# Expert stage of a fused attention, MoE and FFN kernel: queue of the output writes, place of row loads, inner job sizes and banks

## Chip, cores and metric

One core of a Trainium2 chip. The metric is the device time of one execution in microseconds (us). The kernel before takes 1082.27 us, the median of three runs (1080.63 to 1087.08). Engines: TensorE (PE) multiplies matrices, VectorE (DVE), ScalarE (ACT) and GpSimd (POOL) work on elements, SyncE (SP) issues transfers (DMAs); ScalarE and GpSimd can issue them too. Each engine runs its own list of instructions in order and waits on semaphores for the others.

## What is computed

Attention with a window of 128 and 4 sink tokens over 4 x 8 heads of 768 x 64 gives 3072 tokens of 512 values. Each token goes to one of 8 experts, and a second FFN follows:

```python
def _moe_ref(x, w_gate, w1, w2):
    expert_idx = np.argmax(x @ w_gate, axis=1)
    ...  # gate_w: the softmax probability of that expert
    for e in range(8):
        mask = expert_idx == e
        xe = x[mask]
        h = np.maximum(xe @ w1[e], 0.0)          # 512 -> 1024
        out[mask] = gate_w[mask, None] * (h @ w2[e])   # 1024 -> 512
def _moe2_ref(x, w_in, w_out):
    h = x @ w_in                                  # 512 -> 2048
    return (h - np.tanh(h)) @ w_out
```

## The kernel before

Every float32 operand is split into a high and a low float16 half, and a product is three float16 matmuls (`mm3`, L663 to L665).

**Three stages.** Stage A, to about 225 us, is the attention; its rows are scattered by expert into a DRAM tensor `bucket`. Stage B, to about 571 us, runs the experts (`stage_b`). Their outputs go to a DRAM tensor `yc`, ordered by expert, together with the token numbers. Stage C, to the end, runs the FFN over `yc` in six groups of 512 rows; `load_y` (L1041) loads a group transposed into `y`, its token numbers into `idf`.

**Stage B** takes the experts in order of their counts as seen before the last batch, and expert x below is the x-th of that order. Each has a main job over its first rows, `FIRST` = 256 rows for experts 0 to 5 and 128 for 6 and 7. A job is `job()`: layer 1 in blocks of one PSUM bank, each evicted by ScalarE (`h` high, L773) and VectorE (`h` low, L774), then layer 2 into one bank per 128 rows, evicted by L788 and L789, then the output write. The remaining rows are counted in units of 64 and cut into inner jobs under conditionals whose registers are loaded from the table `ctl` (L676): `half` of 64 rows (`half_job`, layer 2 at L813 and L814), `odd` of 128 rows, `jobs` of 256 rows and, behind the first of those, a loop for more. The half and the odd job of an expert run inside its main job's layer 1 (for experts 0 and 1 inside the main jobs of 1 and 2), a 256-row job behind it. The last rows of an expert may be computed twice by overlapping jobs, which write the same values.

**The order around the jobs** is written by hand. `plan(p, f)` puts a step at hook p, and `job` calls `hook(-1)` ahead of its first block, then one hook after each block of layer 1 and each of 8 steps of layer 2. Steps are: register reads and row loads for the next expert (`first`, `decide`, `further_rows`, at the places in `AHEAD`), weights of the next expert (raw chunks `stg` loaded by SyncE, L695 and L699; converted and split by `prep`: L713 on ScalarE, then either L719 on VectorE or L721 and L722 on POOL), pieces of the FFN's weights (`w64_prep`, L742 to L752), and the first `load_y`, at hook `YAT[1]` of expert 6. `both` calls the hook's steps ahead of the inner half or odd job of that place. All stores to `yc` and all row loads are issued by SyncE, in the program's order. A store to `yc` and a later load of it, or the reverse, wait for each other, since the rows are known only at run time.

**Banks.** A main job uses s0 to s3 and pt, pt; a 256-row inner job `MORE` = s1, s2, s3, s0 and oa, ob for layer 2; half and odd jobs `PART` = oa, ob and s0. `soon` gives TensorE a hint on the next branch.

## Time and profile before

| | before |
|---|---|
| median of 3 runs | 1082.27 us |
| profiled execution | 1082.43 us |
| its span | 1080.7 us |
| busy: TensorE, VectorE, ScalarE, GpSimd | 91%, 49%, 40%, 41% |
| mean granted TensorE clock | 0.971 |
| expert stage | about 225 to 571 us |

The span runs from the first to the last instruction. A clock of 1.00 is 2.4 GHz and 0.50 is 1.2 GHz. In rows of a timeline the bracket tells how long the engine was idle before the instruction and which engine, line or transfer released it; `DVEq` or `PEq` is an engine's sequencer (branches, registers), `issue` means that nothing in the trace explains the wait.

### The profile page before, as it was taken

The page shows a single profiled execution, that of the slowest core. Times are in us where ns is not written, and L with a number is a line of the kernel's source. Part 1 is how long each engine was busy: PE and PEld are TensorE (multiplying, and loading weights), DVE is VectorE, ACT ScalarE, POOL GpSimd, SP SyncE. Part 2 cuts the span into 40 slices and gives each one's busy share as a digit, 9 for nine tenths or more (in the row PEclk, how much of TensorE's full clock was granted, in tenths as well). Part 3 has the DMA queues.
Part 4 walks back from the last instruction along what each step waited for, and adds up shares of the span by engine and source line. Part 5 has one row for each costly group of instructions (what it writes and reads, how often), then busy time and mean ns, then how long its engine had stood idle before and what let it go on. Part 6 is the DMA issues. An engine that isn't in the chain of part 4 may idle for free. (4 is left out here: it accounts for less than half of the span.)

```text
span 1080.7 us, 19260 instructions
## 1 busy us (share of the span) xinstructions
PE 986.9 (91%) x6883; PEld 581.0 (54%) x6883; DVE 526.4 (49%) x1188; ACT 428.3 (40%) x1178; POOL 439.7 (41%) x595
## 2 busy tenths in 40 slices
PE   7799878778976999998878999999999999999996
PEld 6688767655654656665543444444444444444442
DVE  6588786846224548574625988352052053043000
ACT  5687776733232334333414563252052043043000
POOL 5777878846203245243412553143143043033010
PEclk9999998998997999999998999999999999999998
DMA  7967788586719877693654415202002000000000
GB/s 195 236 175 202 194 226 229 177 188 220 147 50 268 198 191 220 166 245 127 149 91 81 85 53 147 78 11 49 30 1 50 20 10 11 20 10 1 30 31 20
DMA packets 152264, 125.13 MB, mean 116 GB/s; under 512 B 108800, under 2 KB 121088, under 8 KB 152128
## 3 DMA queue, kind: packets, MB, share of 16 engines
q1 hardware_dynamic: 141616, 94.26, 35.8%
q0 software_dynamic: 8160, 28.34, 8.2%
q8 instruction: 76, 1.25, 0.5%
q10 hardware_dynamic: 2352, 0.79, 0.4%
q14 instruction: 60, 0.49, 0.1%
HBM read 75.98 MB, written 23.79 MB: 92 GB/s over the span
## 5 line engine op out<-in xcount | busy, mean ns | idle before, releaser
L1071 DVE SCALAR_TENSOR_TENSOR w<-z 128x512 f32<-128x512 f32 x96 | 72.6, 756 | 219.7 <-ACT z L1069 215.7
L1059 POOL TENSOR_TENSOR gl<-w,gh 128x512 f16<-128x512 f32 x96 | 117.8, 1228 | 145.6 <-ACT gh L1058 145.2
L663 PE MATMUL s<-y,wi 128*128 128x512 f16 x384 | 146.4, 381 | 6.8 <-DMA y<-yc 6.8
L665 PE MATMUL s<-y,wi 128*128 128x512 f16 x384 | 146.3, 381 | 0.0
L664 PE MATMUL s<-y,wi 128*128 128x512 f16 x384 | 146.3, 381 | 0.0
L663 PE MATMUL pt<-wo,gh 128*128 128x512 f16 x352 | 133.4, 379 | 0.0
L665 PE MATMUL pt<-wo,gl 128*128 128x512 f16 x352 | 133.4, 379 | 0.0
L664 PE MATMUL pt<-wo,gh 128*128 128x512 f16 x352 | 133.4, 379 | 0.0
L1069 ACT ACTIVATE z<-s 128x256 f32<-128x256 f32 x192 | 71.8, 379 | 112.2 <-PE s L665 111.5
L225 PE MATMUL s<-kf,qz 128*128 128x264 f32 (+2 forms) x384 | 100.0, 385 | 3.9 <-DVEq L1279 2.9
L1092 POOL DMA_INDIRECT out_dram<-ot,idu x24 | 23.5, 981 | 196.1 <-ACT ot L1091 186.4
L244 ACT ACTIVATE P<-P,mn 128x264 f32<-128x264 f32 (+1 forms) x192 | 93.6, 489 | 19.5 <-DVE mn L236 18.1
L1091 ACT ACTIVATE ot<-pt 128x512 f32<-128x512 f32 x22 | 13.1, 597 | 194.5 <-PE pt L665 184.7
L731 POOL DMA_DIRECT2D w<-in_w_dram x30 | 16.9, 563 | 149.9 <-DVE f L744 135.6
L225 PEld LDWEIGHTS s<-kf,qz 128*128 128x128 f32 x384 | 66.5, 200 | 11.4 <-PEq L1279 3.2
L1072 DVE SCALAR_TENSOR_TENSOR w<-s,w 128x512 f32<-128x512 f32 x96 | 66.4, 691 | 10.0
L236 DVE CUSTOM_DVE_ANT_0 P<-s,mask 128x264 f32<-128x264 f32 (+1 forms) x192 | 69.5, 396 | 0.9 <-PE s L225 0.6
L268 ACT CAST PT<-pt 128x512 f16<-128x512 f32 (+1 forms) x96 | 52.2, 543 | 36.9 <-PE pt L262 36.5
L663 PEld LDWEIGHTS <-wi 128*128 128x128 f16 x384 | 37.7, 98 | 52.9 <-DVEq L920 7.2
L262 PE MATMUL pt<-ident,P 128*128 128x128 f32 x352 | 60.2, 291 | 6.2 <-DVE PT L274 3.8
L1058 ACT CAST gh<-w 128x512 f16<-128x512 f32 x96 | 59.2, 617 | 11.5 <-DVE w L1072 11.5
L665 PEld LDWEIGHTS <-wi 128*128 128x128 f16 x384 | 37.7, 98 | 45.8 <-issue 1.0
(267 smaller groups left out, 2246.7 us busy)
## 6 DMA issues: line engine op xcount, KB each, us to landing
stg<-in_w_dram SPq DMA_DIRECT2D x64, 512.0 KB
w<-in_w_dram POOLq DMA_DIRECT2D x30, 512.0 KB, 4.4
kf<-in_kT_dram SPq DMA_DIRECT2D x16, 396.0 KB
qz<-in_qT_dram SPq DMA_DIRECT2D x32, 192.0 KB
vf<-in_vP_dram SPq DMA_DIRECT2D x16, 384.0 KB
xf<-xg SPq DMA_DIRECT2D x48, 128.0 KB
row<-hl SPq DMA_DIRECT2D x15, 384.0 KB
yc<-y SPq DMA_DIRECT2D x10, 514.0 KB
```

The source lines that it names most:

```text
L225: nc.tensor.matmul(ps[:, c0:264], lhsT=u.qf[h][:, qc], rhs=u.kf[:, kc], start=True, stop=True, skip_group_check=True)
L236: nc.vector.tensor_tensor_reduce(out=u.P[i // 2][:, it % 4, c0:], in0=s[h][:, c0:264], in1=e.M[:, min(i, 2), c0:], op0=ALU.add, op1=ALU.mi ...
L244: nc.scalar.activation(p, p, AF.Exp, scale=-1.0, bias=u.mn[:, it:it + 1], accum_out=u.sums[:, it:it + 1])
L262: nc.tensor.transpose(ps[:, j], u.P[i // 2][:, it % 4, c0:c0 + 128], e.ident)
L663: nc.tensor.matmul(out, lhsT=lh, rhs=rh, start=start, stop=False)
L664: nc.tensor.matmul(out, lhsT=lh, rhs=rl, start=False, stop=False)
L665: nc.tensor.matmul(out, lhsT=ll, rhs=rh, start=False, stop=stop)
L1058: nc.scalar.copy(gh[:, f], w)
L1059: nc.gpsimd.tensor_tensor(gl[:, f], w, gh[:, f], op=ALU.subtract)
L1069: nc.scalar.activation(z[:, s], p[:, s], AF.Square, scale=1.0 / (YS * WIS), accum_out=e.zsum[:, n:n + 1])
L1071: nc.vector.scalar_tensor_tensor(w, z, -2.5, z, op0=ALU.add, op1=ALU.mult)
L1072: nc.vector.scalar_tensor_tensor(w, p, -2.0 / 15.0 * G2 / (YS * WIS), w, op0=ALU.mult, op1=ALU.mult)
```

## The change

Outputs of the jobs are written by ScalarE's queue (`queue=nc.scalar`), those inside loops still by SyncE; ScalarE therefore reads the registers of the output's place too (`IO`). Expert 2's first rows are loaded in `late`, in job 1, and for later experts at hook 0 of the job before (`AHEAD`). Half job 0 stands at hook 7 of job 1 instead of 5. The steps of a hook come behind the inner job of that place. Experts 4 to 7 (`FEW`) have no 256-row case: their remaining rows are a half job and as many 128-row jobs as needed, from the second on in a loop inside `odd`. Inner 256-row jobs use s2, s3, oa, ob and pt, pt. The first `load_y` stands at hook 1 of expert 6 instead of hook 12. The copy of gate and token number comes before the output's evictions.

```diff
@@ -476,7 +476,8 @@
     nc.vector.tensor_scalar(e.ctl[:, 3], ci[:, 1], 2, None, op0=ALU.logical_shift_right)
-    nc.vector.tensor_scalar(e.ctl[:, 4], ci[:, 1], 1, 1, op0=ALU.logical_shift_right, op1=ALU.bitwise_and)
+    nc.vector.tensor_scalar(e.ctl[:, 4, 0:FEW], ci[:, 1, 0:FEW], 1, 1, op0=ALU.logical_shift_right, op1=ALU.bitwise_and)
+    nc.vector.tensor_scalar(e.ctl[:, 4, FEW:], ci[:, 1, FEW:], 1, None, op0=ALU.logical_shift_right)
     nc.vector.tensor_scalar(e.ctl[:, 8], ci[:, 1], 1, None, op0=ALU.bitwise_and)
@@ -641,14 +642,14 @@
 INNER = "hi", 2
-MORE, PART = (["s1", "s2", "s3", "s0"], ["oa", "ob"]), (["oa", "ob"], ["s0"])
+MORE, PART = (["s2", "s3", "oa", "ob"], OUT), (["oa", "ob"], ["s0"])
 TAIL = [1, 3, 6, 7, 8]
...
 AT = [3, 5]
-YAT = 2, 12
+YAT = 2, 1
 WHEN = [0.0, 0.7, 0.06, 0.7]
 LATER = 0, 256
-AHEAD = [3, 5, 7, 9]
+AHEAD = [0, 5, 6, 7]
 FETCH = (64, 128, 256), (256, 64, 128), (64, 128, 256)
@@ -657,6 +658,10 @@
 ET = mybir.EngineType
+IO = ET.SP, ET.Activation
+FEW = 4
@@ -783,11 +788,11 @@
         e.x64.tile([128, 1, ROW], F16, tag="yo", name="yo", bufs=2)
+    nc.vector.tensor_copy(yr.bitcast(F32)[:, 0:nt, 512:514], g.bitcast(F32)[:, 0:nt])
     for t in range(nt):
...
         nc.vector.scalar_tensor_tensor(yr[:, t, 512:1024], ys[t], gt, yr[:, t, 0:512], op0=ALU.mult, op1=ALU.subtract)
-    nc.vector.tensor_copy(yr.bitcast(F32)[:, 0:nt, 512:514], g.bitcast(F32)[:, 0:nt])
     write(yr)
@@ -815,11 +820,11 @@
     y, gt = yr[0:64, 0], g.bitcast(F32)[0:64, 0, 0:1]
+    nc.vector.tensor_copy(yr.bitcast(F32)[0:64, 0, 512:514], g.bitcast(F32)[0:64, 0])
     nc.scalar.copy(yf, ys[64:128])
...
     nc.vector.scalar_tensor_tensor(y[:, 512:1024], yf, gt, y[:, 0:512], op0=ALU.mult, op1=ALU.subtract)
-    nc.vector.tensor_copy(yr.bitcast(F32)[0:64, 0, 512:514], g.bitcast(F32)[0:64, 0])
     write(yr)
@@ -844,39 +849,39 @@
-    def write(base, start, T):
+    def write(base, start, T, queue=nc.scalar):
         row = nc.s_assert_within(base + start, 0, YROWS - T, skip_runtime_bounds_check_because=WHY)
...
             p = min(T, 128)
-            nc.sync.dma_start(e.yc[bass.ds(row, T), :].rearrange("(t p) c -> p t c", p=p), yr[0:p, 0:T // p].bitcast(U16))
+            queue.dma_start(e.yc[bass.ds(row, T), :].rearrange("(t p) c -> p t c", p=p), yr[0:p, 0:T // p].bitcast(U16))
         return f
...
         for n in names:
-            row, engines, top = dict(n=(1, (ET.SP,), 3072), base=(2, (ET.SP,), 3072), jobs=(3, None, 12),
-                                     odd=(4, None, 1), done=(5, (ET.SP,), 256), s1=(6, (ET.SP,), 3072 - 256),
-                                     so=(7, (ET.SP,), 3072 - 128), half=(8, None, 1), sh=(9, (ET.SP,), 3072 - 64))[n]
+            row, engines, top = dict(n=(1, (ET.SP,), 3072), base=(2, IO, 3072), jobs=(3, None, 12),
+                                     odd=(4, None, 1 if x < FEW else 24), done=(5, (ET.SP,), 256), s1=(6, IO, 3072 - 256),
+                                     so=(7, IO, 3072 - 128), half=(8, None, 1), sh=(9, IO, 3072 - 64))[n]
             setattr(regs[x], n, w.reg(row, x, engines, top))
...
-        load_regs(x, "n", "base", "done", "s1", "so", "sh")
+        load_regs(x, "base", "so", "sh", *(("n", "done", "s1") if x < FEW else ()))
         if x >= 2:
...
-        load_regs(x, "jobs", "odd", "half")
+        load_regs(x, "half", "odd", *(("jobs",) if x < FEW else ()))
...
         r, i = regs[x], x % 2
-        if T == 256:
+        if T == 256 and x < FEW:
             load_x(x, xi[i], gi[i][:, 1], r.s1, T)
-        elif T == 128:
+        if T == 128:
             load_x(x, xo[i], go[i], r.so, T)
-        else:
+        if T == 64:
             load_x(x, e.xh[i], e.gh[i], r.sh, T)
@@ -902,7 +907,7 @@
         tc.mark_branch_hint_location(f"{which}{x}", hint=dict(half=lambda: r.half >= 1, odd=lambda: r.odd >= 1, jobs=lambda: r.jobs >= 1,
-                                                              more=lambda: r.jobs >= 2)[which](), engines=(ET.PE,))
+                                                              more=lambda: (r.jobs if x < FEW else r.odd) >= 2)[which](), engines=(ET.PE,))
@@ -911,12 +916,25 @@
         r, i = regs[x], x % 2
+        def hook(p):
+            if p == 5 and x >= FEW:
+                soon(x, "more")
         with tc.If(r.odd >= 1, label=f"odd{x}"):
-            job(nc, e, w.parts(x), xo[i], go[i], 128, *PART, lambda p: None, write(r.base, r.so, 128),
-                INNER)
+            job(nc, e, w.parts(x), xo[i], go[i], 128, *PART, hook, write(r.base, r.so, 128), INNER)
+            if x >= FEW:
+                with tc.If(r.odd >= 2, label=f"more{x}"):
+                    with tc.For_i(1, r.odd) as k:
+                        at = nc.s_assert_within(FIRST[x] + 128 * (k - 1), 0, 3072 - 128,
+                                                skip_runtime_bounds_check_because=WHY)
+                        load_x(x, xo[i], go[i], at, 128)
+                        job(nc, e, w.parts(x), xo[i], go[i], 128, *PART, lambda p: None,
+                            write(r.base, at, 128, nc.sync), INNER)
...
         r, i = regs[x], x % 2
+        if x >= FEW:
+            return
         with tc.If(r.jobs >= 1, label=f"jobs{x}"):
@@ -924,7 +942,7 @@
                     job(nc, e, w.parts(x), xi[i], gi[i][:, 0], 256, *MORE, lambda p: None,
-                        write(r.base, start(x, k), 256))
+                        write(r.base, start(x, k), 256, nc.sync))
@@ -966,12 +984,13 @@
                         w.load(2, c)
+        first(2)
     plan(AT[0], late)
...
         plan(AT[1] + c // 2, *w.prep(2, c, "ap" if c % 2 else "ad"))
-    plan(4, lambda: soon(0, "half"))
-    plan(5, lambda: half(0))
-    plan(6, lambda: soon(0, "odd"))
+    plan(6, lambda: soon(0, "half"))
+    plan(7, lambda: half(0))
+    plan(8, lambda: soon(0, "odd"))
     plan(9, lambda: odd(0))
@@ -979,7 +998,6 @@
     soon(1, "jobs")
-    first(2)
     for c in range(2):
@@ -994,7 +1012,7 @@
             plan(AHEAD[0], lambda: first(x + 1))
-            plan(AHEAD[0], lambda: decide(x + 1))
+            plan(AHEAD[1], lambda: decide(x + 1))
             for k, t in enumerate(FETCH[2]):
@@ -1020,7 +1038,6 @@
         def both(p):
-            hook(p)
             if p == -1:
@@ -1028,8 +1045,9 @@
                     soon(inner[points[k]][1], inner[points[k]][0].__name__)
-            if p == n + (6 if x == 2 else 3):
+            if p == n + (6 if x == 2 else 3) and x < FEW:
                 soon(x, "jobs")
+            hook(p)
         job(nc, e, w.parts(x), first_rows(x), gs[x % 2][:, 0:T // 128], T, FOUR, OUT, both, write(regs[x].base, 0, T))
```

SyncE's list behind job 0's 256-row inner job, in the kernel before: expert 2's rows (`xs`, `gs`), FFN weights (`w`), then expert 3's raw weights (`stg`).

```order
L920 UNCONDITIONAL_BRANCH
L676 TENSOR_LOAD ctl x5
L842 ISA
L842 DMA_TRANSPOSE xs_328<-bucket 128x8x256
L844 ISA
L844 DMA gs_330<-bucket 128x2x4
L731 DMA w_5639<-in_w_dram 128x1024
L731 DMA w_5641<-in_w_dram 128x1024
L676 TENSOR_LOAD ctl
L695 ISA
L695 DMA stg<-in_w_dram 128x1024
```

The same place of the changed kernel:

```order
L938 UNCONDITIONAL_BRANCH
L736 DMA w_5652<-in_w_dram 128x1024
L736 DMA w_5654<-in_w_dram 128x1024
L681 TENSOR_LOAD ctl
L700 ISA
L700 DMA stg<-in_w_dram 128x1024
```

The rows of expert 2 now stand ahead of half job 0 in SyncE's list, and the loads of weights follow the inner job at once.

ScalarE's list at the start of expert 2, in the changed kernel: `w_320<-stg` is the first preparation for expert 3, `h<-s` are evictions of expert 2's layer 1, L813 those of half job 1, L753 is a cast of an FFN weight.

```order
L718 ACTIVATE w_320<-stg 128x1024
L778 ACTIVATE h<-s_6086 128x512
L681 TENSOR_LOAD ctl x4
L753 ACTIVATE wi_4784<-f_6073 128x512
L718 ACTIVATE stg<-stg 128x1024
L778 ACTIVATE h<-s_6152 128x512
L914 COMPARE_AND_BRANCH
L813 ACTIVATE h<-oa 128x4x64
L813 ACTIVATE h<-ob 128x4x64
L824 COPY h<-s_6284 64x512
L826 ACTIVATE yo<-h,gh_4797 64x512
L857 ISA
```

Before, a third preparation and a second cast stood ahead of the half job, and three register reads behind it; the output write that now follows was SyncE's.

SyncE's list in expert 6, in the kernel before: the first `load_y` (L1041, L1042) stands behind the loads for expert 7 and expert 6's output.

```order
L844 DMA go_4344<-bucket 128x4
L842 ISA
L842 DMA_TRANSPOSE xi_4340<-bucket 128x8x256
L844 ISA
L844 DMA gi_4342<-bucket 128x2x4
L852 ISA
L852 DMA yc<-yo 128x1028
L1041 DMA_TRANSPOSE y_4785<-yc 128x8x512
L1042 DMA idf<-yc 128x4x4
```

The same list in the changed kernel, from the end of expert 6's conditional 128-row case:

```order
L923 UNCONDITIONAL_BRANCH
L1059 DMA_TRANSPOSE y_4786<-yc 128x8x512
L1060 DMA idf<-yc 128x4x4
L681 TENSOR_LOAD ctl x2
L847 ISA
L847 DMA_TRANSPOSE xh_4794<-bucket 128x8x64
```

The load now stands ahead of those for expert 7's half and odd jobs, and no output write of expert 6 is ahead of it in this list.

## Rows read from the trace of the kernel before

**Rows 1.** TensorE's waits from 210 to 600 us: line and releaser, total, times, longest.
```profile
PE s L663 <- DMA gs<-bucket: 11.1, 1, 11.1
PE s L813 <- DVE h L809: 9.4, 4, 3.9
PE s L663 <- DMA y<-yc: 6.8, 1, 6.8
PE s L663 <- DVEq L923: 5.9, 3, 2.2
...
PE s L663 <- DVEq L920: 3.7, 2, 1.9
PE oa L663 <- POOL y L721: 2.8, 1, 2.8
PE pt L664 <- issue: 1.8, 1, 1.8
...
PE pt L663 <- issue: 1.5, 2, 1.3
```

**Rows 2.** Timeline of TensorE: start, duration, matmul, idle before it and its releaser.
```profile
329.04 0.37 PE L663 MATMUL s<-xs,y 128*128 128x256 f16 x1 [11.14 <-DMA gs<-bucket]
...
342.91 0.61 PE L813 MATMUL s<-w,h 128*128 128x512 f16 x1 [3.92 <-DVE h L809]
...
529.99 0.23 PE L663 MATMUL s<-xs,w 128*128 128x128 f16 x1 [1.91 <-DVEq L920]
...
551.08 0.23 PE L663 MATMUL s<-xs,w 128*128 128x128 f16 x1 [1.75 <-DVEq L920]
...
570.90 0.58 PE L663 MATMUL s<-y,wi 128*128 128x512 f16 x1 [6.79 <-DMA y<-yc]
```

**Rows 3.** Stretches of TensorE: length, busy time, granted clock, DMA share, GB/s.
```profile
329.04:336.16 7.12, 7.12 (x53) 0.75 0.99 353
404.70:410.10 5.40, 5.40 (x48) 1.00 0.54 182
507.10:512.10 5.00, 4.99 (x17) 0.71 0.42 141
570.89:575.30 4.41, 4.40 (x12) 0.55 0.17 62
```

**Rows 4.** The tile ctl: reads of one register, ns min/median/max.
```profile
L676 ACTq TENSOR_LOAD <-ctl x24: 272/278/465, 265.1 to 546.5; - x24
```

**Rows 5.** Timeline of SyncE's issues, end of job 0 to expert 2.
```profile
319.74 0.38 SPq L852 DMA_DIRECT2D yc<-y  x1
324.54 2.23 SPq L842 DMA_TRANSPOSE xs<-bucket  x1
...
327.48 0.94 SPq L731 DMA_DIRECT2D w<-in_w_dram  x2
328.94 2.37 SPq L695 DMA_DIRECT2D stg<-in_w_dram  x4
```

**Rows 6.** Timeline of ScalarE at the start of expert 2.
```profile
334.84 1.06 ACT L713 ACTIVATE w<-stg 128x1024 f16<-128x1024 f32 x1 [10.64 <-DMA stg<-in_w_dram]
335.80 0.58 ACT L773 ACTIVATE h<-s 128x512 f16<-128x512 f32 x1
336.28 0.62 ACT L748 ACTIVATE wi<-f 128x512 f16<-128x512 f32 x1
```

**Rows 7.** Groups by line, 225 to 571 us: busy us, mean ns, idle before.
```profile
L809 DVE SCALAR_TENSOR_TENSOR h<-oa,h 128x256 f16<-128x256 f32 x5 | 2.1, 417 | 8.4 <-ACT h L808 8.4
...
L789 DVE SCALAR_TENSOR_TENSOR yo<-s,go,yo 128x512 f16<-128x512 f32 x2 | 1.5, 750 | 9.1 <-ACT yo L788 9.1
```

**Rows 8.** Timeline of SyncE's issues, end of the expert stage.
```profile
544.24 0.57 SPq L852 DMA_DIRECT2D yc<-yo  x1
...
559.92 0.37 SPq L852 DMA_DIRECT2D yc<-yo  x1
562.78 4.16 SPq L1041 DMA_TRANSPOSE y<-yc  x1
```

## The prediction

> **What bounds the kernel now.** I read the page first. TensorE is busy for 91% of the span (the table above), so a saving must be time in which TensorE idles or runs at the lower clock. The diff touches the expert stage alone (about 225 to 571 us). There the table of TensorE's waits is the list of what can be won: 11.1 us for the first rows of expert 2, 9.4 us in four waits for a half job's activations, 6.8 us for the first load of the FFN's input, and 5.9 plus 3.7 us in which TensorE waits for VectorE to get past a conditional [rows 1]. The timeline shows the larger ones in place [rows 2]. The table of stretches adds what a wait leaves behind: after three long waits the granted clock is 0.75, 0.71 and 0.55 on average, so that many of the matmuls run at 1.2 instead of 2.4 GHz, and after a wait of 2.2 us it is 1.00 [rows 3]. TensorE is busy throughout these stretches, so what a low clock costs is the missing share times the length: 0.25 × 7.12 = 1.8 us behind the first, 0.29 × 5.00 = 1.5 behind the second, 0.45 × 4.41 = 2.0 behind the third.
>
> The expert counts of this input follow from the jobs that run. Expert 4 has 193 rows left after its main job. Before, these are one inner job of 256 rows; after, `odd` is 2 for it, and they are two jobs of 128 rows, the second inside the loop. Experts 5 and 6 take a half job, expert 7 nothing.
>
> **The change part by part** (gains +, losses −, us).
>
> *(a) Job 1 and half job 0: −0.9.* ScalarE now reads 18 instead of 6 registers in front of the preparation of expert 2's weights; one read is 0.278 us [rows 4], so 12 more are 3.3 us. TensorE already waits 2.8 us there for POOL's part of that preparation [rows 1]. The half job is placed two steps later (12 matmuls; 4.41 × 0.55 = 2.4 us for as many at full clock [rows 3]). The wait becomes 2.8 + 3.3 − 2.4 = 3.7. Bounds: +1 (the reads lie in idle time) to −3 (nothing of them is covered, and the clock falls).
>
> *(b) Start of expert 2: +5.2.* Before, SyncE issues job 0's output at 319.74, can go on only when it has landed (324.54, 4.8 us later), then loads expert 2's rows, and TensorE starts at 329.04 after a wait of 11.14 us [rows 2, 5]. After, these rows come some 30 us earlier, in job 1. That wait goes, and its clock loss. But something else is late next: the raw weights of expert 3, whose first preparation stands on ScalarE ahead of expert 2's evictions. Before, that preparation started at 334.84 after waiting 10.64 for its load [rows 6], issued at 328.94 [rows 5], 5.9 us earlier. In the changed program SyncE's loads in front of it wait for the completion slot of job 0's output, which ScalarE issues at about 319.6 and which by the same 4.8 us lands at 324.4. Two loads (0.94 [rows 5]) and a register read later the weights are issued (325.6) and land at 331.5. From there ScalarE needs two preparations of 1.05, two evictions of 0.60, four register reads of 0.28, a cast of 0.62, and the half job two activations and one VectorE operation of 0.42 each: 2.1 + 1.2 + 1.1 + 0.6 + 1.3 = 6.3 [rows 4, 6, 7]. So the second layer of half job 1 starts near 337.7 instead of 342.91 [rows 2]: +5.2. TensorE's work till there ends near 326.3 (317.9, plus 5.4 for expert 2's first half, plus 3.0), so it waits some 11 us in front of it and runs slowly behind it, as it did before. Bounds: +3 (landings 2 us later) to +15 (the weights are no longer late).
>
> *(c) Inner jobs on other banks: +4.1.* Behind the inner 256-row jobs of experts 2 and 3 TensorE waited 2.2 and 1.85 us for VectorE to leave the conditional (three such waits, 5.9 in all [rows 1]): the next job's first bank is also a bank of the inner job's loop. Now the inner job and its loop use other banks, which the next job needs 5 us later. What remains is TensorE's own branch, which I take to be nothing. Bounds: +2 to +4.1.
>
> *(d) Expert 4: −4.1.* Two jobs of 128 rows stream as many columns as one of 256 and are counted equal. Won are the third 1.85 us wait behind an inner job and a stall of 1.8 us some matmuls after TensorE jumps over the 128-row case [rows 1]: +3.7. New is the loop. Its rows are loaded while the first job's second layer runs, so hidden if the load takes its usual time. At the loop's end every engine waits for all others and for the loop's own output write: ScalarE and VectorE 0.75 each by VectorE's row [rows 7], issue and landing 2.86 (559.92 to 562.78, where SyncE waits for just such a write [rows 8]), and for the joins 1.4 as an estimate, a little under the 1.85 that leaving one conditional took [rows 1]: 5.8. Behind it the clock is down: 2.0. Sum −4.1. The trace of before has no executed loop; the lower bound is −12, by the nearest chain of write, load and start, 11.14 [rows 2], the upper −1 (only operations and landing, no clock loss).
>
> *(e) Half job 5 and the next start: +4.9.* In front of the half job's second layer VectorE did planned preparation first; the hook now stands behind the half job. The wait there is one of the four that make 9.4 [rows 1]; it is the one ahead of the 0.71 stretch and 2.99 us long. It shrinks to a chain of the three operations of 0.42, about 1.4 (+1.6), the clock stays up (+1.5 [rows 3]), and 1.91 us for VectorE at the start of expert 6 goes, since no 256-row case stands there any more [rows 2]: +5.0, less 0.1 for branches. Bounds +2 to +5.
>
> *(f) Experts 6, 7 and the FFN's first rows: +10.1.* From expert 6's first matmul (529.99) to the FFN's (570.90) 40.9 us pass [rows 2]. The load was issued at 562.78, behind expert 6's output [rows 8] and the loads for expert 7, and TensorE waited 6.79 us and then lost 2.0 to the clock [rows 2, 3]. Now it stands in expert 6's first layer, right behind the half job. That job's output was issued 14.25 us after expert 6's start (544.24 [rows 8]); 0.6 sooner and 2.86 for the landing give +16.5, and 8.1 for the load (562.78 to 570.90) +24.6. TensorE needs until then: expert 6 without its 1.75 wait at the end and 0.6 of its half job's (551.08 − 529.99 − 2.35 = 18.7) and expert 7 (570.90 − 6.79 − 551.08 = 13.0): +31.7. So the load is hidden, with 7 us to spare. Its price: expert 6's output, now on ScalarE, must wait for that load, since both touch one tensor, and ScalarE's evictions for expert 7 wait behind it until +24.6, some 1 us too late. 40.9 − 32.8 + 2.0 = +10.1. Bounds: +6 to +11.
>
> *Moving the writes* costs ScalarE one issue each, 0.38 us by the first of [rows 5]; about 17 run, and each holds ScalarE until VectorE's last operation, 0.75 [rows 7]. In a layer of 256 rows ScalarE has one eviction of 0.60 per 2.7 us [rows 3, 6], so I count nothing. Without that cover it is 17 × 1.1 = 19 us. The copy that moves forward is no longer than an eviction and counts nothing.
>
> Sum: −0.9 + 5.2 + 4.1 − 4.1 + 4.9 + 10.1 = **+19.3**. The profiled execution took 1082.43 (span 1080.7 and 1.7 around it), next to the median of 1082.27: 1082.4 − 19.3 = **1063.1, say 1063 us**.
>
> **The rivals.**
> 1. *ScalarE held by its writes (the other side).* Each write waits for an earlier one's landing and holds the evictions behind it. For: a landing took 4.8 us [rows 5], and evictions feed every layer. Against: most writes stand at a job's end, with a layer before the next bank is needed. If each of the 17 stops TensorE for 1.1 us, nothing is won; from 1.8 us on the kernel is over 1% slower, at 1093.
> 2. *Expert 3's weights aren't late at expert 2.* Then half job 1's second layer follows its own chain (326.3 + 1.3 = 327.6) or comes a few us after it: 5 to 10 more, about 1055. For: SyncE's loads need not share that slot for long. Against: the changed program's list of waits names it.
> 3. *The FFN's load isn't hidden,* because the half job's output or this load is held past +32: (f) falls away, 1082.4 − 9.2 = 1073. For: the load took 8.1 us in a quieter place. Against: 7 us to spare.
> 4. *Longer jumps.* Over the 128-row cases of experts 5, 6 and 7 TensorE now jumps past twice the code, since the loop is inside. Before, one such jump was followed by a stall of 1.8 us without a releaser, another by 1.3 [rows 1]. If all three stall for 1.8, 5.4 is lost: 1068. The Trainium skill's page "Runtime: NRT & Kernel Launch" (Instruction fetch mechanics) says that a taken branch out of the prefetched pages stalls until the target is fetched; by that these stalls stay or grow. The trace agrees only in part: other jumps over the same case show none.
> 5. *Waits only replaced:* each shortened wait comes back at the next late thing; about 1080. For: (a) and (b) show two such. Against: behind (c), (e) and (f) I find no successor over 1 us.
>
> **How the numbers follow.** Forecast 0.48 (its own range 1058 to 1067), rival 2 0.13, rival 3 0.11, rival 4 0.11, rival 5 0.10, rival 1 0.07. The range 1051 to 1074 takes in the forecast and rivals 2 to 4 but for their tails: 0.8. One per cent, about what a measurement of this kernel can tell from no change, is 10.8 us, so faster means under 1071.5. Faster: 0.48 + 0.13 + 0.11, some of rival 3 and a little of 5 make 0.78; same 0.17; slower 0.05.
>
> **What would show it.** Right: no wait on `gs<-bucket` at expert 2, but one of 8 to 11 us on VectorE's `h` at half job 1, with ScalarE waiting for `stg` before it; no waits on VectorE's branch behind experts 2, 3 and 5; one of about 6 us at the start of expert 5 with a clock below 1.00 behind it; none on `y<-yc`, and the FFN starting near 553. Wrong: waits on evictions spread over all jobs, or `y<-yc` still there.

## The result, and the profile of the changed kernel

The changed kernel takes 1074.88 us (median of 20 runs, 1066.31 to 1080.83), the kernel before beside it 1084.05 (20 runs, 1079.00 to 1091.04). The ratio is 0.9912, with a 95% interval of 0.9889 to 0.9935: a gain of 9.5 us (7 to 12) where 19.3 were forecast. It lies just above the forecast's range, and the sign was right. The profiled execution took 1078.94 us (span 1077.1), 4 us more than the median, so it shows a little more trouble than most executions have. The second profile with the same order of work, of the experiment e3_y12 below, took 1069.37, and where the two differ that is said. Two executions, one of the kernel before (2061.53 us, beside e1 to e4) and one of e7 (1175.74), were far slower than all others of their kernel and stand in no ratio.

The table of TensorE's waits in the changed kernel, from 210 to 600 us: line and releaser, total, times, longest.

```profile
PE pt L668 <- ACT stg L718: 8.5, 1, 8.5
PE s L668 <- ACT w L718: 7.6, 1, 7.6
PE s L818 <- DVE h L814: 6.9, 4, 2.9
PE pt L668 <- PEq L923: 5.1, 3, 3.5
...
PE s L670 <- DVE h L779: 3.1, 2, 1.8
...
PE s L668 <- ACT h L778: 2.8, 1, 2.8
```

The 11.1 for `gs<-bucket`, the 6.8 for `y<-yc` and the waits for VectorE's branches [rows 1] are gone, as forecast. The first two rows here, the fourth and the last two are new. The same waits stand in TensorE's timeline (start, duration, matmul, idle before it and its releaser):

```profile
290.20 0.61 PE L668 MATMUL s<-w,h 128*128 128x512 f16 x1 [2.76 <-ACT h L778]
...
328.23 0.37 PE L668 MATMUL s<-xs,y 128*128 128x256 f16 x1 [7.60 <-ACT w L718]
...
340.72 0.39 PE L818 MATMUL s<-w,h 128*128 128x512 f16 x1 [2.85 <-DVE h L814]
...
358.84 0.39 PE L670 MATMUL s<-w,h 128*128 128x512 f16 x1 [1.77 <-DVE h L779]
...
403.69 0.27 PE L668 MATMUL s<-xs,w 128*128 128x256 f16 x1 [0.74 <-ACT y L794]
...
489.37 0.61 PE L668 MATMUL pt<-w,h 128*128 128x512 f16 x1 [8.47 <-ACT stg L718]
...
561.08 0.59 PE L668 MATMUL pt<-w,h 128*128 128x512 f16 x1 [3.46 <-PEq L923]
...
568.99 0.38 PE L668 MATMUL s<-y,wi 128*128 128x512 f16 x1
```

What each of them leaves behind, by the table of stretches (length, busy time, granted clock, DMA share, GB/s):

```profile
290.05:296.90 6.85, 6.70 (x24) 0.75 0.57 124
328.08:334.91 6.83, 6.68 (x49) 0.78 0.94 330
340.56:345.88 5.32, 5.16 (x17) 0.68 1.30 338
...
489.21:502.40 13.19, 13.03 (x48) 0.78 1.05 253
560.92:568.90 7.98, 7.82 (x24) 0.64 0.01 2
568.90:573.30 4.40, 4.40 (x22) 1.00 0.16 60
```

The last line is the FFN's start, which was at 0.55 before [rows 3].

Three groups of TensorE's own branches (engine, operation, count, ns min/median/max, first and last start) show where it had to jump: L923 ends the cases of 128 rows, L927 the loop in expert 4's, L938 the cases of 256 rows.

```profile
L923 PEldq COMPARE_BRANCH  x10: 75/254/4443, 278.1 to 556.5; - x10
...
L927 PEldq COMPARE_BRANCH  x3: 76/227/3110, 466.6 to 486.2; - x3
...
L938 PEldq COMPARE_BRANCH  x4: 67/76/4902, 295.8 to 421.5; - x4
```

For the comparisons below I took, in TensorE's timeline of each profiled execution, the first matmul of each expert's main job (for job 0 the first of the stage) and list the time from one to the next, in us:

| section | before | changed | e3 | e1 | e2 | e6 | e5 | e11 | e12 |
|---|---|---|---|---|---|---|---|---|---|
| jobs 0 and 1 to expert 2 | 103.9 | 103.1 | 100.6 | 100.8 | 96.5 | 97.4 | 97.0 | 97.4 | 95.6 |
| expert 2 to 3 | 75.7 | 75.5 | 77.2 | 77.1 | 70.4 | 71.1 | 69.0 | 71.0 | 68.2 |
| expert 3 to 4 | 44.6 | 43.4 | 43.5 | 43.5 | 43.4 | 43.4 | 43.4 | 43.6 | 43.5 |
| expert 4 to 5 | 46.6 | 55.3 | 52.1 | 43.5 | 62.4 | 54.8 | 45.1 | 44.3 | 46.2 |
| expert 5 to 6 | 34.1 | 27.6 | 27.4 | 28.1 | 27.5 | 27.5 | 28.1 | 28.1 | 28.1 |
| experts 6, 7 to FFN | 40.9 | 38.9 | 35.9 | 38.8 | 37.6 | 36.2 | 37.7 | 40.8 | 38.8 |
| sum | 345.8 | 343.9 | 336.7 | 331.7 | 337.9 | 330.5 | 320.4 | 325.3 | 320.3 |

Three sections fell short of the forecast: the first two together (1.0 us won where (a), (b) and the first wait of (c) had 6.5), expert 4, which lost 8.7 us where 4.1 were forecast, and experts 6 and 7 (2.0 won where 8.1 were forecast, the FFN's clock apart). One profile is thin ground for a few us: the stage's first matmul comes between 219.4 and 225.8 us in the 14 profiles, although no edit acts ahead of it.

### The profile page after: what moved, and what is told of

The parts are those of the page before. It is cut to its first block, busy times and chain, and to the rows that moved or that the text cites. A ratio compares the mean times of both kernels' runs of the same rounds, so it can differ in the third digit from the quotient of the medians.

```text
span 1077.1 us, 19456 instructions
## 1 busy us (share of the span) xinstructions
PE 988.2 (92%) x6979; PEld 581.9 (54%) x6979; DVE 528.3 (49%) x1190; ACT 427.3 (40%) x1178; POOL 437.8 (41%) x595
## 5 line engine op out<-in xcount | busy, mean ns | idle before, releaser
L244 ACT ACTIVATE P<-P,mn 128x264 f32<-128x264 f32 (+1 forms) x192 | 93.6, 489 | 19.3 <-DVE mn L236 17.5
L668 PE MATMUL pt<-w,h 128*128 128x512 f16 x160 | 63.7, 398 | 15.6 <-ACT stg L718 8.5
L726 POOL TENSOR_SCALAR w<-stg 128x1024 f16<-128x1024 f32 x25 | 29.1, 1164 | 91.6 <-ACT stg L718 72.2
```

The costliest lines, as they stand in the source:

```text
L244: nc.scalar.activation(p, p, AF.Exp, scale=-1.0, bias=u.mn[:, it:it + 1], accum_out=u.sums[:, it:it + 1])
L668: nc.tensor.matmul(out, lhsT=lh, rhs=rh, start=start, stop=False)
```

## The experiments

Each is an edit of the changed kernel; each ratio is to the kernel before, run beside it on the same chip (medians of before: 1081.67 for e1 to e4, 1080.35 for e5 to e8, 1079.36 for e9 to e12). The changed kernel itself stands at 0.9912. The fences show changed lines, with `...` between places; those of e7, e8 and e9 show the step from e5, e7 and e8.

### Four suspects apart: e1 to e4

**e1_few8** gives experts 4 to 7 their 256-row case back, so that no loop runs and the 128-row cases are short.

```diff
-FEW = 4
+FEW = 8
...
-    nc.vector.tensor_scalar(e.ctl[:, 4, FEW:], ci[:, 1, FEW:], 1, None, op0=ALU.logical_shift_right)
```

> The changed kernel with the 256-row case back for experts 4 to 7 (no loop runs for expert 4, the 128-row cases are short again); all else as changed. Theory J (jumps and the loop): in the trace of the changed kernel TensorE waits 8.47 us behind expert 4's loop, 5.3 of them for the loop's end and 3.1 in the jump out of it, and then runs at a lower clock (13.2 us for a second layer instead of 10.5); it waits 1.25 and 3.46 us behind jumps over the longer 128-row cases of experts 6 and 7, and 2.6 more for the clock. All of this goes, at most 2 us come back for jumps over the 256-row cases: 15 to 18 us faster than the changed kernel, ratio to the kernel before 0.975 to 0.979. Rival H (ScalarE held by output writes is what delays experts 6 and 7): only the loop's part goes, 9 to 11 us, ratio 0.981 to 0.984, and the 3.46 us wait in expert 7 stays. Rival: the loop costs no more than the waits that the 256-row case brings back; ratio 0.990.

Measured: 1066.04 us, 0.9868 [0.9829, 0.9908]. Expert 4's section falls to 43.5 us, so the loop costs 11.8 us by this pair of profiles and 8.6 against e3's. Experts 6 and 7 gained next to nothing (38.8 against 38.9, and 35.9 in e3). With shorter cases of 128 rows TensorE jumps over cases of 256 rows in their place, and its branch at their end (L937 here) is as long. In experts 6 and 7 TensorE waits 2.1 us behind these branches, by its table of waits, and 3.0 and 1.5 us at two places for which the trace names no releaser:

```profile
L937 PEldq COMPARE_BRANCH  x8: 67/884/5009, 290.6 to 550.0; - x8
...
PE pt L667 <- issue: 3.0, 1, 3.0
PE s L667 <- PEq L937: 2.1, 3, 0.8
```

The theory that the loop costs is borne out; the theory that doubled cases are what makes experts 6 and 7 slow is not. Over all profiles these two take 36 to 40 us with the loop's code in their cases and 37 to 41 without it (e10, which waits for the load, left out).

**e2_spw** puts the writes back on SyncE's queue.

```diff
-    def write(base, start, T, queue=nc.scalar):
+    def write(base, start, T, queue=nc.sync):
```

> The changed kernel with all output writes back on SyncE's queue (ScalarE still reads the registers). Theory H1 (half job 0's write, which waits 6.7 us on ScalarE for a row load to land, holds the evictions of the 128-row job 0): the 2.76 us wait there and some 1.5 us of clock go, and SyncE, held by its writes again, loses little elsewhere: 2 to 5 us faster than the changed kernel, ratio 0.987 to 0.989. Rival Q (the queue move is what brings the gain, since SyncE's loads no longer stand behind writes): 5 us or more slower than the changed kernel, ratio 0.996 or more, with new waits on loads of rows or weights.

Measured: 1070.96 us, 0.9904 [0.9871, 0.9938], no better as a whole. But the first two sections are 11.6 us shorter than in the changed kernel, and expert 4's is 7.1 longer. Its table of waits names the reason:

```profile
PE oa L668 <- DMA xo<-bucket: 6.9, 1, 6.9
```

SyncE's issues there, the write of the 128-row job and behind it the load of the loop's rows:

```profile
460.17 0.38 SPq L857 DMA_DIRECT2D yc<-yo  x1
461.70 1.29 SPq L847 DMA_TRANSPOSE xo<-bucket  x1
```

With the write in front, the loop's rows are asked for only once the first job has its output, and TensorE waits 6.9 us for them. So ScalarE's queue is worth something for the loop and costs something in front of it; with the loop gone both should be had (e5).

**e3_y12** leaves the FFN's first load where the kernel before had it, and all else as changed.

```diff
-YAT = 2, 1
+YAT = 2, 12
```

> The changed kernel with the first load of the FFN's input back at hook 12 of expert 6. Theory S (slack): expert 6's output leaves ScalarE near 554.4 and lands by 557.3, the load takes 8.1 us and lands near 565.4, before TensorE has finished expert 7 at 568.9; so the place alone brings nothing, and what removed the wait on this load is that expert 6's output no longer stands behind four row loads on SyncE: ratio 0.990 to 0.993, no wait on y<-yc or one under 1 us. Rival P (the place is what removed the wait): 6 to 9 us slower than the changed kernel, ratio 0.997 to 1.000, a wait on y<-yc of 4 us or more and a low clock at the FFN's start.

Measured: 1070.87 us, 0.9915 [0.9883, 0.9947], the same as the changed kernel. The load is issued at 550.87 instead of 546.55 and TensorE waits 0.3 us for it. Its earlier place is not what hides it; e10 tests what does.

**e4_noj1** leaves out the code of expert 1's 256-row case and its hint. With these counts that case runs no job, so only the jump over it goes.

```diff
-    soon(1, "jobs")
...
-    jobs(1)
```

> The changed kernel without the code of expert 1's 256-row case, which does not run on these counts (the hint on it goes too). TensorE's jump over it took 4.9 us in the changed kernel and ended the 7.6 us wait at the start of expert 2. Theory W (expert 3's raw weights decide when half job 1's second layer can start, as the prediction had it): expert 2 starts near 320.5, but half job 1's second layer starts at 339 to 341 as before, behind a wait of some 11 us: 0 to 2 us faster than the changed kernel, ratio 0.989 to 0.992. Rival J2 (the jump decides): all 7.6 us and 1.4 us of clock are won, ratio 0.982 to 0.984.

Measured: 1071.43 us, 0.9908 [0.9875, 0.9941]. The jump's wait at expert 2 falls from 7.60 to 2.28, and the half job behind it takes what is won (first TensorE's timeline, then ScalarE's):

```profile
318.20 0.37 PE L668 MATMUL s<-xs,y 128*128 128x256 f16 x1 [2.28 <-DVEq L941]
...
335.64 0.61 PE L818 MATMUL s<-w,h 128*128 128x512 f16 x1 [7.65 <-DVE h L814]
```

```profile
328.83 1.06 ACT L718 ACTIVATE w<-stg 128x1024 f16<-128x1024 f32 x1 [4.33 <-DMA stg<-in_w_dram]
```

The jump of 4.9 us is real, and at this place it costs nothing: the weights of expert 3 are later than it is.

### The sum of both, and the half jobs' writes: e5, e6, e11, e10

**e5_few8_spw** is e1 and e2 together.

> The changed kernel with two parts undone: the 256-row case is back for experts 4 to 7, and all output writes are on SyncE. Each alone was measured: 0.987 and 0.990, the second with 4 us won in job 1, 7 us won in expert 2, and 7 us lost in expert 4, where the loop's row load stood behind a write in SyncE's list. Theory A (the writes on ScalarE cost about 11 us in job 1 and expert 2, and the loss in expert 4 needs the loop): without the loop the two add up, expert stage near 321 us, 20 us or more faster than before, ratio 0.974 to 0.979. Rival B (SyncE held by its writes costs elsewhere what ScalarE gains): ratio 0.985 to 0.990.

Measured: 1054.98 us, 0.9766 [0.9737, 0.9795]. The first two sections keep what e2 won and expert 4 what e1 won, as the theory that the two add up had it.

**e6_halfsp** moves only the half jobs' writes back to SyncE; the loop stays.

```diff
-write(r.base, r.sh, 64))
+write(r.base, r.sh, 64, nc.sync))
```

> The changed kernel with the output writes of the half jobs alone on SyncE; all others stay on ScalarE. Theory H2 (it is half job 0's and half job 1's writes, in the middle of a main job, that wait on ScalarE in front of the 128-row jobs' evictions): the waits in layer 2 of the 128-row jobs 0 and 1 (0.5 to 2.8 and 1.8 to 3.3 us) go, expert 2 is 3 to 7 us shorter, no 6.9 us wait for rows in expert 4's loop: 5 to 9 us faster than the changed kernel, ratio 0.983 to 0.987. Rival (any write on ScalarE costs, the half jobs' no more than the others): 0 to 3 us, ratio 0.988 to 0.992, and those waits stay.

Measured: 1061.75 us, 0.9832 [0.9803, 0.9862], 0.0080 or 8.7 us below the changed kernel. Five of the 19 writes that run from ScalarE in the changed kernel's expert stage are moved by it. By the profiles the gain lies in the first two sections (10.0 us together); the others stay within 0.6 us, but for experts 6 and 7 with 2.7, a section in which e3's profile differs by as much. In its table of waits the row of 2.8 for `h` is gone, and these two are smaller than the changed kernel's 6.9 and 3.1:

```profile
PE s L818 <- DVE h L814: 5.3, 4, 1.7
...
PE s L670 <- DVE h L779: 1.3, 1, 1.3
```

What the writes did there is in the next section, under *Moving the writes*.

**e11_few8_halfsp** is e1 and e6 together.

> As e6_halfsp (0.983: half jobs' writes on SyncE, the others on ScalarE), with the 256-row case back for experts 4 to 7. Theory A: the loop's cost goes here too, 11 to 14 us: ratio 0.971 to 0.974. Against e5_few8_spw (0.9766) it tells whether the other writes are better on ScalarE's queue than on SyncE's: the theory that ScalarE's queue is worth nothing but where it holds nobody gives the same within 2 us; if SyncE's waits for results had cost, e11 is 3 to 5 us faster.

Measured: 1055.10 us, 0.9759 [0.9734, 0.9784], the same as e5. Whether the other writes stand on SyncE's or ScalarE's queue makes no difference that can be measured. Against e6 the loop's removal brings 0.0073, 7.9 us.

**e10_spw_y12** is e5 with the FFN's load at its old place, so that expert 6's output is written from SyncE ahead of it, as in the kernel before.

> As e5_few8_spw (0.9766: 256-row case for all experts, all writes on SyncE), with the first load of the FFN's input back at hook 12 of expert 6, as in the kernel before; the row loads for expert 7 stay at their earlier places. Moving the place alone, with the writes on ScalarE, had changed nothing (e3). Theory O (either is enough: expert 6's output away from SyncE, or the load ahead of it in SyncE's list): with both undone the wait on y<-yc comes back, 4 to 8 us and a low clock at the FFN's start, ratio 0.981 to 0.986. Rival R (it was the earlier row loads of expert 7 that cleared SyncE's list): no wait over 1 us, ratio 0.975 to 0.978.

Measured: 1059.59 us, 0.9801 [0.9775, 0.9827], 3.8 us over e5, a little less than expected, and the intervals of the two overlap. The old wait is back in the table of waits, and SyncE's issues show the order:

```profile
PE s L667 <- DMA y<-yc: 6.8, 1, 6.8
```

```profile
538.21 0.37 SPq L856 DMA_DIRECT2D yc<-yo  x1
541.28 4.36 SPq L1058 DMA_TRANSPOSE y<-yc  x1
```

So either edit hides the load: the write off SyncE's queue (e3) or the load in front of the write (e5). The change makes both, and one would have done.

### The start of expert 2: e7, e8, e9, e12

**e7_few8_spw_swap** is e5 with the empty case of expert 1 ahead of expert 0's case, so that its jump and the jump behind the inner job are not both paid at expert 2.

```diff
-    plan(10, lambda: soon(0, "jobs"))
+    plan(10, lambda: soon(1, "jobs"))
...
+    jobs(1)
+    soon(0, "jobs")
     jobs(0)
-    soon(1, "jobs")
...
-    jobs(1)
```

> As e5_few8_spw, and expert 1's 256-row case stands ahead of expert 0's in the program instead of behind it, so that TensorE jumps over it (it does not run) while matmuls of job 1 are still queued, and not with an empty queue in front of expert 2. Theory J (a jump costs what the queued matmuls don't cover): the 7.6 us wait at the start of expert 2 shrinks to 1 us or less, and the low clock behind it goes; half job 1's second layer then waits for expert 3's weights, so that about 2 to 5 us are won against e5: ratio lower by 0.002 to 0.005. Rival (the wait at expert 2's start is not the jump but ScalarE's preparations that it follows in the trace): the wait stays, ratio as e5.

Measured: 1055.98 us, 0.9778 [0.9742, 0.9813], nothing won. TensorE's wait at expert 2 is 2.4 instead of 7.7, and half job 1's is 7.0: as in e4.

**e8_few8_spw_swap_w3** also loads expert 3's raw weights earlier, in job 1.

```diff
-    for c in range(4):
-        w.load(3, c)
     decide(2)
...
+    plan(10, lambda: [w.load(3, c) for c in range(4)])
```

> As e7_few8_spw_swap, and expert 3's raw weights are loaded in job 1 instead of behind expert 0's 256-row job. Theory W (their landing decides when half job 1's second layer starts, once the jump is out of the way): that layer waits 3 us or less, and expert 2 ends 4 to 9 us sooner than in e7: ratio lower than e7's by 0.004 to 0.008. Rival (ScalarE's four preparations behind expert 0's job decide): the wait stays at 5 us or more, ratio as e7 within 0.002.

Measured: 1053.84 us, 0.9765 [0.9735, 0.9795]. The half job still waits 5.3 us, now behind a cast of an FFN weight on ScalarE:

```profile
325.38 0.63 ACT L752 ACTIVATE wi<-f 128x512 f16<-128x512 f32 x1 [5.56 <-DVE f L748]
```

**e9_early** loads that FFN weight earlier too, and keeps ScalarE from reading the counts' registers that it no longer needs.

```diff
-IO = ET.SP, ET.Activation
+IO = (ET.SP,)
...
-    for c in range(2):
-        w64_load(nc, e, c, nc.sync)
...
-    plan(10, lambda: [w.load(3, c) for c in range(4)])
+    plan(10, lambda: [w.load(3, c) for c in range(4)] + [w64_load(nc, e, c, nc.sync) for c in range(2)])
```

> As e8_few8_spw_swap_w3 (0.9765), and the first two pieces of the FFN's weights are loaded in job 1 too, and ScalarE no longer reads registers that only SyncE's writes need. In e8 the 5.3 us wait in front of half job 1's second layer no longer ended with expert 3's weights but with a cast on ScalarE that waited 5.6 us for VectorE's work on such a piece. Theory L (layers: each cause that is removed uncovers the next, and this is the last one at this place): that wait falls to 2 us or less, expert 2 ends 4 to 8 us sooner, ratio 0.968 to 0.973. Rival (there is another late thing right behind, so that expert 2 gains less than 2 us): 0.975 to 0.978.

Measured: 1054.67 us, 0.9769 [0.9737, 0.9800], and the wait is 7.0. The theory that late loads hold the half job falls: in this trace no engine waits for a load ahead of it, and what is left is the preparation itself. VectorE's timeline shows it, first beside GpSimd's operations, then without them:

```profile
319.67 2.35 DVE L746 TENSOR_SCALAR f<-w 128x512 int32<-128x512 int32 x1
322.05 1.41 DVE L747 SCALAR_TENSOR_TENSOR f<-w,f 128x512 int32<-128x512 int32 x1
323.49 2.49 DVE L748 SCALAR_TENSOR_TENSOR f<-w,f 128x512 int32<-128x512 int32 x1
...
327.64 0.41 DVE L746 TENSOR_SCALAR f<-w 128x512 int32<-128x512 int32 x1
328.09 0.69 DVE L747 SCALAR_TENSOR_TENSOR f<-w,f 128x512 int32<-128x512 int32 x1
328.82 0.69 DVE L748 SCALAR_TENSOR_TENSOR f<-w,f 128x512 int32<-128x512 int32 x1
```

```profile
318.76 2.98 POOL L726 TENSOR_TENSOR w<-stg,w 128x1024 f16<-128x1024 f32 x1
321.70 1.22 POOL L725 TENSOR_SCALAR w<-stg 128x1024 f16<-128x1024 f32 x1
323.01 2.43 POOL L726 TENSOR_TENSOR w<-stg,w 128x1024 f16<-128x1024 f32 x1
```

**e12_early_noswap** is e9 without the swap, so that the jump over expert 1's empty case stands at expert 2 again, with all loads early.

> As e9_early, but expert 1's 256-row case in its old place, right in front of expert 2, so that TensorE jumps over it with an empty queue. In e5, e7 and e8 the jump's 5 to 7 us lay beside the wait for weights and cost nothing. Theory J (with the weights early the jump is what ends last): a wait of 6 to 8 us at the start of expert 2 with a low clock behind it, 5 to 9 us slower than e9. Rival: the same as e9 within 2 us, since something else still ends later than the jump.

Measured: 1049.78 us, 0.9718 [0.9694, 0.9742]: the fastest of all, ahead of both kernels by 29.6 us (before) and some 21 (changed, by the ratios). My expectation, that the jump's wait would come on top, was wrong. TensorE's timeline:

```profile
314.95 0.37 PE L667 MATMUL s<-xs,y 128*128 128x256 f16 x1 [7.72 <-ACT w L717]
...
325.21 0.39 PE L817 MATMUL s<-w,h 128*128 128x512 f16 x1 [0.44 <-DVE h L813]
```

VectorE and GpSimd prepare while TensorE jumps, and the half job then waits 0.44 us: the preparation takes its time in either order, and here the jump lies beside it. From the end of job 0's inner job to half job 1's second layer 18.0 us pass here (307.23 to 325.21) and 17.8 in e9 (312.71 to 330.50); it is 17.7 in e8, 17.9 in e7, 18.8 in e5 and 20.1 in the changed kernel. So the early loads won 0.1 us at their place behind the swap and 0.9 without it, and e12's lead does not come from there.

Why e12 comes out 5 us under e9 and e5 isn't settled. From job 0 to expert 3 the profiles of e9 and e12 differ by 4.8 us (168.6 against 163.8): 3.3 lie ahead of that stretch, 1.6 of them a wait of e9 at the jumped case that the swap moved there (291.69). In experts 6 and 7, where neither edit acts, lie 2.2 more. Against e5 the profiled stage is equally long (320.3), and e12's lead of 4.8 in the span lies outside it: its stage starts at 219.36 instead of 225.78.

## Why the prediction was wrong, step by step

**What bounds the kernel: right.** Where an edit moved a section, TensorE's waits and the clock behind them moved with it. What lies outside, such as e12's lead over e5, no edit here explains.

***Moving the writes*, counted at nothing: the step that failed most.** The working was that a write holds ScalarE until VectorE's last operation. For 17 of the 19 writes (the working had about 17 in all) that holds exactly: in the changed kernel's trace each leaves 0.03 us behind that operation. The other two, of half jobs 0 and 1, leave 6.2 and 1.5 us behind it, since they also wait for row loads on SyncE's queue. ScalarE's timeline at these two:

```profile
280.87 0.72 ACT L826 ACTIVATE yo<-h,gh 64x512 f16<-64x512 f32 x1 [0.75 <-DVE h L825]
288.59 0.60 ACTq L857 DMA_DIRECT2D yc<-yo  x1
289.55 0.60 ACT L778 ACTIVATE h<-oa 128x512 f16<-128x512 f32 x1 [7.96 <-issue]
...
350.43 0.51 ACTq L857 DMA_DIRECT2D yc<-yo  x1
351.14 0.63 ACT L753 ACTIVATE wi<-f 128x512 f16<-128x512 f32 x1 [3.02 <-DMA go<-bucket]
```

and SyncE's, the first row at half job 0, the other two for (b) and (f) below:

```profile
281.64 2.90 SPq L847 DMA_TRANSPOSE xi<-bucket  x1
...
328.49 1.64 SPq L700 DMA_DIRECT2D stg<-in_w_dram  x1
...
546.55 4.20 SPq L1059 DMA_TRANSPOSE y<-yc  x1
```

The half job's output was ready at 282.4, when VectorE had done its part, and its write left at 288.59. In the trace's list of who waited for the tile `xi`, whose load SyncE issued at 281.64, ScalarE's `h` stands with 8.0 us:

```profile
who waited for it (us, times):
  ACT h L778: 8.0, 1
```

The write and this load have no tensor in common: one goes from `yo` to `yc`, the other from `bucket` to `xi`. What they share is a completion slot, the semaphore on which a transfer reports its landing. In the trace's records the write's wait ends on the semaphore on which it will report itself, and the report before its own there is that of `xi`, at 288.43, 0.16 us before the write leaves. The same pair meets in the traces of e1, e3 and e4. The working of (b) reckons with just such a slot on SyncE's side (its loads wait for the slot of job 0's output, and so they do: landed 327.04, next load issued 327.06); for the writes themselves it was not asked for.

Behind the write stood the evictions of the 128-row job, and TensorE waited 2.76 us for them (290.20) with the clock at 0.75 behind it, 0.25 × 6.85 = 1.7 us more. At half job 1 ScalarE stands for 3.0 us, and TensorE for 1.77 (358.84). The row names `go`, but the write left at 350.43 and `go` landed at 351.34; the slot is that of `xh`, whose load landed at 350.20. The rival for the other side had this mechanism, "holds the evictions behind it", but as 1.1 us at each of 17 places; it was two places, in the first two sections, and they cost 8.7 us by e6 (11.8 by e1 and e11). How much of it falls on which place changes from one execution to the next: in e3's profile ScalarE stands for 5.69 us at the first and TensorE only for 0.49, but at the second TensorE waits 0.39 and 2.92 us, and that layer takes 10.1 us where e6's takes 5.3. No run gave the two writes another slot on ScalarE's queue, so that they would then have left in time is read from the traces and not tried.

***(d)* Expert 4's loop: the mechanism right, the term mis-sized.** The working was a wait of 5.8 and 2.0 for the clock, less 3.7 won: −4.1. The row says 8.47 us, in two parts: all engines are through at 486.2, 5.3 us after TensorE, which is the 5.8 (the loop's write, issued at 482.43, lands at 485.49); and then TensorE's branch out of the loop, which starts at 486.2, takes 3.11. The row's releaser, ScalarE's `stg`, is not what ended it: the same branch was over by 486.1 on the other engines. The clock behind it is 0.78 over 13.19 us, 2.9 instead of 2.0, since a whole second layer follows. A wait of 1.3 us in the first 128-row job adds to it (`DVE h L779`, second of 2). So 5.3 + 3.1 + 2.9 + 1.3 − 3.7 = 8.9, and 8.7 was measured. In e3's profile the wait is 5.4, without the long branch, and the section 52.1, a loss of 5.4: nearer to the forecast, and still short. By whole runs the loop costs 4.8 us (e1 against the changed kernel) to 7.9 (e11 against e6); the 14.9 of e5 against e2 hold the late row load too. The intervals of these differences are 4 to 5 us wide on either side.

***(f)* Experts 6 and 7: the load right, the sum 6 us too high.** The load was issued at 546.55, near where the working put it, and the FFN starts at 568.99 without a wait and at 1.00. But the section is 38.9 instead of 32.8. What is missing, 6.1, is mostly in the fourth row of the table of waits: two of its three waits for TensorE's own branch L923 lie here, 1.25 and 3.46 us (the branch takes up to 4.4), and behind the longer one the clock is 0.64 over 7.98 us (2.9). Together that is 7.6, a little more than is missing. This is the rival of longer jumps, at its place: it had 5.4 us in three stalls, the three waits of the row make 5.1, and the clock comes on top. The Trainium skill's page "Runtime: NRT & Kernel Launch" (Instruction fetch mechanics) has it that a taken branch out of the prefetched pages stalls until its target is there; these rows of 3.1, 4.4 and 4.9 us agree with it, and by the median of 0.25 most jumps are not of that kind, but what was prefetched no run here shows. The rival's reason fell: e1 halves the jumped cases and is no faster here. Jumps over the cases of 256 rows, as long, take their place, together with 4.5 us of waits without a releaser; what causes those stays open.

***(c)* The banks: +2.6 instead of +4.1.** The three waits for VectorE's branch are gone; TensorE's own way out of the conditional, counted at nothing, leaves 0.74 behind expert 2 and 0.75 behind expert 3, in both cases with the matmul 0.36 us behind the branch's end (2.22 − 0.74 + 1.85 − 0.75 = 2.6). The third of them belonged to (d).

***(a)* −0.9: measured −2.7,** but not for the register reads: it is the write of half job 0 above. Counted from the stage's first matmul, job 0's inner job ends within 0.3 us of where it did before in the profiles of e1, e3 and e4, where TensorE waits 0.5 to 1.0 us behind the write, and 3.1 us sooner in e6, with the write on SyncE and 15 of the 18 reads still there.

***(b)* The start of expert 2: +5.2, measured +4.9, and right in its mechanism.** The next late thing was `stg`, as said: issued at 328.49, 7.9 us after job 0's inner job (7.7 in the working, 325.6 after 317.9), with ScalarE's preparation waiting for it:

```profile
334.54 1.06 ACT L718 ACTIVATE w<-stg 128x1024 f16<-128x1024 f32 x1 [5.37 <-DMA stg<-in_w_dram]
```

From the end of job 0's inner job (328.23 − 7.60) to half job 1's second layer (340.72) 20.1 us pass, before 25.0 (329.04 − 11.14 to 342.91 [rows 2]); in e1, e2 and e3 it is 20.0 to 20.1 too. The wait of 8 to 11 us that was to show it came apart: 7.60 at expert 2 for TensorE's jump of 4.9 us and what follows it, 2.85 at the half job. e4 shows that the jump ran beside the late weights, and e8, e9 and e12 that with the weights early this stretch still takes 17.7 to 18.0 us. The rival of weights that aren't late is thus answered: it would have brought some 2 us here, not 5 to 10.

***(e)* +4.9: measured +6.5.** The wait in front of expert 5's half job and the one at the start of expert 6 are both gone.

**The other rivals.** That the FFN's load isn't hidden fell with its row; the price it would have had is some 3.8 us by e10, with overlapping intervals. That waits are only replaced was half true: at expert 2 and in experts 6 and 7 a successor took part of each gain, and the time fell between this rival's 1080 and the forecast.

**The sum.** By place, in this profile: −2.7 + 4.9 − 2.7 (half job 1's write and the waits behind it, up to expert 3) + 2.6 − 8.7 + 6.5 + 4.0 = +3.9, and 1082.43 − 1078.94 = 3.5. With the half jobs' writes back on SyncE the kernel comes to 0.9832 of before; the forecast's 1063.1 is 0.9822 of 1082.4. That the two are so near is in part luck: in e6 the terms (d) and (f) are still too high (expert 4 loses 8.1 us there), and the first two sections win 11 us where the forecast had 6.5.

## What to carry to other kernels

A write that is moved to a compute engine's queue takes its place in that engine's program, with every wait that it needs: list for each moved transfer what it waits for, among it earlier transfers on any queue that report on the same semaphore, and what stands behind it, before counting it at nothing. A loop that runs once instead of a larger job costs its exit (all engines, the last write, the jump, and the clock on what follows), here 5 to 8 us for 128 rows. When a wait goes, look for the next late thing twice: behind the late load here stood a late FFN weight, and behind that the preparation itself, so that loading both earlier won less than 1 us at that place.

## What the runs showed that was not expected

- TensorE's branches took 0.07 to 4.9 us in the changed kernel's expert stage, those of the other engines 0.08 at most. The long ones cost nothing where something else was later (e4); where nothing was, the branch of 4.4 us left TensorE idle for 3.46, with a low clock behind it (561.08).
- VectorE's short integer operations took 2.35, 1.41 and 2.49 us beside GpSimd's, and 0.41, 0.69 and 0.69 without. In each row VectorE ends 0.3 to 0.5 us after the operation of GpSimd that was running when it began (318.76 + 2.98 = 321.74 and 319.67 + 2.35 = 322.02). The Trainium skill's page "SBUF — State Buffer" (Who interferes with whom) describes a pair of ports that the two share and that one of them holds for a whole instruction; these rows agree with it.
- The changed kernel and e3, whose edit acts only at the end of the stage, differ by 9.4 us in their profiled spans: 2.4 lie ahead of the expert stage (its first matmul at 225.14 and 222.78), 7.1 in it, and there up to expert 2 (2.5 us), in expert 4 with the loop's exit (3.3) and in experts 6 and 7 (2.9), with 1.7 the other way between experts 2 and 3. One profile of each is thin ground for a difference of 3 us; the ratios over whole runs decided here.
